# Sending sixteen rows of one load through half of the DMA engines, and riding small inputs in larger transfers

## The chip, the core and the metric

The kernel runs on one core of a Trainium2 chip. The core has a matrix engine (PE, with its weight loads listed apart as PEld), a vector engine (DVE), a scalar engine (ACT), GpSimd (POOL) and a synchronisation engine (SP), and 16 DMA engines that bring data from the chip's memory (HBM) into the on-chip memory (SBUF, 128 partitions or "rows"). Here SP issues nearly all loads, ACT issues three small ones. The metric is the device time of one execution in microseconds (us). The kernel before takes 699.19 us, the median of three runs (698.89 to 699.32).

## The reference

One decode step of a transformer block, all in float32, with batch 2, one query token per sequence, model width 512, 32 heads of 128, a key and value cache of 4096 positions, and a feed-forward layer of width 1376:

```python
mod = (silu(c) @ w_mod).reshape(2, 6, 1, 512)
sa, ca, ga, sb, cb, gb = (mod[:, i] for i in range(6))
h = layernorm(x) * (1 + ca) + sa
q = (h @ wq)                                  # 32 heads
p = softmax(q . k_cache / sqrt(128))
x = x + ga * ((p . v_cache) @ wo)
h = layernorm(x) * (1 + cb) + sb
x = x + gb * (mish(h @ w1 + b1) @ w2)
```

The caches are 2 x 32 x 4096 x 128 floats each, so that K and V together are 268 of the 297 MB that are read. Everything else is weights (wq and wo 8.4 MB each, w_mod 6.3 MB, w1 and w2 2.8 MB each) and a few kilobytes of vectors.

## The kernel before, in words

**Loads.** On the host the inputs are laid out as a list of loads, `stream()`, and each load is an array of 128 rows. K of one head is 8192 columns (32 KB a row), V of one head the same. Three buffers in SBUF take the loads in turn: two of the tag `two` (16384 columns) and one of the tag `one` (12288 columns). The first load (lines 46 and 143) holds the first three modulation weights `m012` and the first two pieces of `wq`, in two transfers. Then K and V come head by head, mostly two heads in one transfer, with a piece of `wq` or `wo` beside every fifth head. The last three loads are cut into smaller transfers (lines 59 to 63): the last piece of `wo` with the fourth modulation `m4`, then V of the last head in three cuts; the third modulation `m3` and `w1` in two halves; `m5` and `w2` in four cuts, the last two of 512 columns (2 KB a row).

**What sets the order.** The order of instructions on each engine is written out by hand. `used(...)` (line 148) issues the next load as soon as the code that reads its buffer's former contents has been written, and at run time the transfer waits on semaphores until those readers are done. A transfer also waits for the transfer that used the same of the eight DMA semaphores eight transfers earlier. All loads stand in SP's one queue.

**Work per head.** DVE multiplies K by q (line 316) and sums (line 319), PE and DVE find the maximum over all rows (lines 324 to 337), ACT takes the exponential (line 339), and PE multiplies by V (line 365, `weighted_v`). V runs behind K by some heads. After four heads the sums are normalised (`head_values`) and multiplied by a piece of `wo` (`project_o`).

**The start.** ACT issues three small transfers of its own, c and x (8 rows each, line 165) and the biases b1 as 128 rows of 12 floats (line 167). PE transposes c (`columns`, line 231), then a matmul at line 263 puts the biases into the accumulator `fps`, and the modulation matmuls follow (`modulation`, line 241).

**The tail.** After the last head's V the attention output is completed (lines 486 to 494), the second normalisation is computed (`centred`, line 194, and `rstd`, line 215), and around it PE computes the modulation `m3` in two halves (lines 499 and 502) and a few idle matmuls (`busy`, line 293), whose result nobody reads. Then follow w1 (line 521), the activation (lines 548 to 556), w2 (line 561), two DVE operations (lines 569 and 570) and the store of the result (line 571).

Of the kernel before, what the change touches and what calls it, by code (L numbers as in the profile page):

```python
# [8 lines left out]
F32 = mybir.dt.float32  # L9
# [4 lines left out]
P = 128  # L14
WIDTHS = (384, 384, 352, 256)
CHUNKS = [(g, j) for j in range(3) for g in range(4) if WIDTHS[g] > P * j]
HEADS = 32
HC = 4
BIG = 8192
W = 2048  # L20
SIZES = {
    "k": BIG, "v": BIG, "wq": W, "wo": W, "m012": 3 * W, "m3": W, "m4": W, "m5": W,
    "w1": 4 * sum(WIDTHS), "w2": 512 * len(CHUNKS),
}
AHEAD = (14, 22)


def stream():

    behind, pieces = {}, [("k", 0)]
    for h in range(1, HEADS):
        pieces.append(("k", h))
        if h not in AHEAD:
            behind[h] = len(behind)
            pieces.append(("v", behind[h]))
    left = list(range(len(behind), HEADS))
    pieces += [("v", h) for h in left[:-1]]

    extra = {}
    for c in range(2, HEADS // HC):
        at = (pieces.index(("k", HC * c)) - 1) // 5 * 5
        extra[at] = [("wq", c), ("wo", c - 2)]
    extra[60] = [("wo", HEADS // HC - 2)]
    loads = [[([("m012", 0), ("wq", 0), ("wq", 1)], (3 * W, 2 * W))]]
    n = 0
    while n < len(pieces):
        m = 1 if n % 5 == 0 else 2
        keys = pieces[n : n + m]  # L50
        if keys[0] == ("v", left[0]) and m == 2:
            loads.append([([key], (BIG,)) for key in keys])
        else:
            keys = keys + (extra.pop(n, []) if m == 1 else [])
            loads.append([(keys, (sum(SIZES[kind] for kind, _ in keys),))])
        n += m
    assert not extra and len(loads) % 3 == 0
    last = HEADS - 1
    loads += [
        [([("wo", HEADS // HC - 1), ("m4", 0)], (2 * W,)), ([("v", last)], (BIG // 2, BIG // 4, BIG // 4))],  # L60
        [([("m3", 0), ("w1", 0)], (W, 2 * sum(WIDTHS), 2 * sum(WIDTHS)))],
        [([("m5", 0), ("w2", 0)], (W, 6 * 512, 3 * 512, 512, 512))],
    ]
    return loads, behind, left
# [3 lines left out]
def kernel(  # L68
# [1 line left out]
    tc: tile.TileContext,  # L70
    loads: list,
    head: bass.AP,
    b1c: bass.AP,
    behind: dict,
    left: list,
    out: bass.AP,
# [9 lines left out]
    nc = tc.nc  # L86
    ctx.enter_context(tc.manual_schedule())
    B = 2
    DH = 128
    D = 512  # L90
    G = D // P
    R = P // G
    TB = R // B
    H = HEADS
    NS = BIG // (B * DH)
    NJ = 3
    EPS = 1e-5
    SCALE = DH ** -0.5
    NCH = len(CHUNKS)

    const = ctx.enter_context(tc.tile_pool(name="const", bufs=1))
    work = ctx.enter_context(tc.tile_pool(name="work", bufs=2))
# [18 lines left out]
    def take(t, keys):  # L121
        lo = 0
        for kind, n in keys:
            part = t[:, lo : lo + SIZES[kind]]
            lo += SIZES[kind]
            if kind in "kv":
                (k_t if kind == "k" else v_t)[n] = part.rearrange("p (b j d) -> p b j d", b=B, d=DH)
            elif kind in ("wq", "wo"):
                (wq_t if kind == "wq" else wo_t)[n] = part.rearrange("p (k n) -> p k n", k=G)
            else:  # L130
                w_t[kind] = part.rearrange("p (k n) -> p k n", k=NCH if kind == "w2" else G)

    w_t = {}
    done = set()

    def load(n):

        t = room(n)
        lo = 0
        for keys, srcs in loads[n]:  # L140
            take(t[:, lo:], keys)
            for src in srcs:
                nc.sync.dma_start(out=t[:, lo : lo + src.shape[-1]], in_=src)  # L143
                lo += src.shape[-1]

    loaded = 0
# [1 line left out]
    def used(*keys):  # L148

        nonlocal loaded  # L150
        done.update(keys)
        while loaded < len(loads) and (
            loaded < 3 or all(key in done for keys, _ in loads[loaded - 3] for key in keys)
        ):
            load(loaded)
            loaded += 1
# [1 line left out]
    used()  # L158


    cq = work.tile([P, P], F32, tag="xn", name="cq", bufs=1)
    xq = const.tile([P, P], F32, name="xq")
    for t, src in ((cq, head[0]), (xq, head[1])):
        nc.gpsimd.memset(t, 0.0)
        nc.scalar.dma_start(out=t[::TB, :], in_=src)
    bias = const.tile([P, NCH + 1], F32, name="bias")
    nc.scalar.dma_start(out=bias, in_=b1c)
    nc.scalar.preload_act_table_set("natural_log_exp_and_others")
    ident = const.tile([P, P], F32, name="ident")
    make_identity(nc, ident)  # L170
# [3 lines left out]
        out=fold, in_=ident.rearrange("p (g r) -> p r g", g=G), axis=AX.X, op=ALU.add  # L174
# [3 lines left out]
        out=mean_w, in0=fold[:, None, :].to_broadcast([P, G, R]), scalar1=1.0 / D, scalar2=None, op0=ALU.mult  # L178
# [55 lines left out]
    def modulation(name, n, t, ps=None, ks=range(G)):  # L234


        if ps is None:
            ps = wide_ps(f"modps{name}")[:, : n * P].rearrange("p (m n) -> p m n", m=n)
        for k in ks:
            for g in range(G):  # L240
                nc.tensor.matmul(  # L241
                    ps[R * g : R * (g + 1)],
                    lhsT=ct[:, k, :],
                    rhs=t[:, k, :].rearrange("p (m n) -> p m n", m=n)[:, :, P * g : P * (g + 1)],
                    start=(k == 0),
                    stop=(k == G - 1),
                )
        return ps
# [8 lines left out]
    xn = work.tile([P, P], F32, tag="xn", name="xn", bufs=1)  # L257
    xc, var, rs = centred(xq, "a")
# [1 line left out]
    nc.vector.tensor_scalar(out=xn, in0=xc, scalar1=y0, scalar2=y1, op0=ALU.mult, op1=ALU.mult)  # L260

    fps = psum.tile([P, 512], F32, tag="att2", name="fps", bufs=1)[:, : NJ * G * B]
    nc.tensor.matmul(fps, lhsT=ident, rhs=bias[:, :, None].to_broadcast([P, NJ * G, B]), start=True, stop=False, skip_group_check=True)  # L263

    ps = modulation("0", 3, w_t["m012"])
    hq = const.tile([P, P], F32, name="hq")
# [1 line left out]
    nc.vector.tensor_tensor(out=hq, in0=ps[:, 0, :], in1=hq, op=ALU.add)  # L268
    mod = {}

    def keep(m, ps):
        mod[m] = const.tile([P, P], F32, name=f"mod{m}")
        nc.scalar.copy(mod[m], ps)

    keep(2, ps[:, 2, :])
    hps = columns(hq, "hps")
    hc = const.tile([P, G, B], F32, name="hc")
    nc.vector.tensor_copy(hc, hps)  # L278
# [14 lines left out]
    def busy(n):  # L293

        for lo in range(0, n, 2):
            cols = P * min(2, n - lo)
            nc.tensor.matmul(ov[1][:, :cols], lhsT=ident, rhs=e_t[0][0].rearrange("p c m -> p (c m)")[:, :cols], start=True, stop=True)
# [130 lines left out]

    project_q(0)
    project_q(1)  # L430
    used(("m012", 0), ("wq", 0), ("wq", 1))
    for h in range(H):
        products(h)
        if h:
# [61 lines left out]
    def add_x(total):  # L496
        nc.vector.scalar_tensor_tensor(x2, xg, 1.0, xq, op0=ALU.mult, op1=ALU.add, accum_out=total)

    mps3 = modulation("3", 1, wm3, ks=(0, 1))

    def more_work():
        modulation("3", 1, wm3, mps3, (2, 3))
        busy(1)

    xc, var, rs = centred(x2, "b", add_x, more_work)
    busy(6)
    nc.vector.tensor_tensor(out=m4, in0=xc, in1=m4, op=ALU.mult)
    y0, y1 = rstd(var, rs)
    nc.scalar.activation(xc, m4, AF.Copy, scale=y0)
# [37 lines left out]

    nc.vector.tensor_scalar(out=f[:, 0], in0=hid, scalar1=30.0, scalar2=None, op0=ALU.min)
    nc.scalar.activation(f[:, 0], f[:, 0], AF.Exp)
    keep(5, gps[:, 0, :])  # L550
    busy(6)
    nc.vector.scalar_tensor_tensor(f[:, 1], f[:, 0], 2.0, f[:, 0], op0=ALU.add, op1=ALU.mult)
    nc.vector.tensor_scalar(out=f[:, 2], in0=f[:, 1], scalar1=2.0, scalar2=None, op0=ALU.add)
# [20 lines left out]
def _lay_out(np, a):  # L574


    def rows(w):

        return w.reshape(-1, P, w.shape[-1]).transpose(1, 0, 2)

    def q_rows(v):

        return v.reshape(2, 4, P).transpose(1, 0, 2).reshape(8, P)

    B, H, S, DH = a["A_k_cache"].shape
    kv = {
        kind: a[n].reshape(B, H, P, -1).transpose(1, 2, 0, 3).reshape(H, P, -1)
        for kind, n in (("k", "A_k_cache"), ("v", "A_v_cache"))
    }
    wq = rows(a["A_wq"]).reshape(P, 4, 8, 512).transpose(2, 0, 1, 3).reshape(8, P, -1)  # L590
    wo = a["A_wo"].reshape(8, 4, P, 512).transpose(0, 2, 1, 3).reshape(8, P, -1)
    wm = rows(a["w_mod"])
    w1 = rows(a["B_w1"])
    starts = np.cumsum((0,) + WIDTHS)
    b1c = np.zeros((P, 12), a["B_b1"].dtype)
    w2 = np.zeros((P, len(CHUNKS), 512), a["B_w2"].dtype)
    for n, (g, j) in enumerate(CHUNKS):
        f0 = starts[g] + P * j
        f1 = min(f0 + P, starts[g + 1])
        b1c[: f1 - f0, n] = a["B_b1"][f0:f1]  # L600
        w2[: f1 - f0, n] = a["B_w2"][f0:f1]

    pieces = {**kv, "wq": wq, "wo": wo, "m012": [wm[:, :, :1536]], "w1": [w1], "w2": [w2]}
    for n in (3, 4, 5):
        pieces[f"m{n}"] = [wm[:, :, 512 * n : 512 * (n + 1)]]
    arrays = {
        "head": np.stack([q_rows(a["c"]), q_rows(a["A_x"])]),
        "b1c": b1c,
    }
    for n, parts in enumerate(stream()[0]):  # L610
        for i, (keys, widths) in enumerate(parts):
            row = np.concatenate([pieces[kind][m].reshape(P, -1) for kind, m in keys], axis=1)
            cuts = np.split(row, np.cumsum(widths)[:-1], axis=1)
            for j, t in enumerate(cuts):
                arrays[f"load{n}_{i}_{j}"] = np.ascontiguousarray(t)
    return arrays
# [24 lines left out]
```

## Time and profile before

| | |
|---|---|
| median of three runs | 699.19 us |
| the profiled execution's own time | 698.83 us |
| its span, first to last instruction | 697.0 us |
| DVE busy | 595.8 us (85%) |
| PE busy | 308.2 us (44%) |
| ACT busy | 43.7 us (6%) |
| read from HBM | 297.22 MB, 426 GB/s over the span |

The profiled execution is 1.8 us longer than its span (what lies before the first and after the last instruction), and 0.36 us shorter than the median of the runs. In the windows and pages quoted below, "DMA share" is the mean busy share of the 16 DMA engines: 1.00 means that all 16 had a packet under way all of the time. A packet of a load is one row of it. Queue q1 carries what SP issues, q10 what ACT issues, and the rows marked "instruction" carry the engines' own program.

### The profile page before, as it was taken

What the parts mean: (1) busy time and instruction counts of PE and PEld (TensorE: products, weight loads), DVE (VectorE), ACT (ScalarE), POOL (GpSimd) and SP (SyncE); (2) the same over time, 40 slices, a digit from 0 to 9 for tenths busy, and PEclk for the clock granted to TensorE, in tenths of its full rate; (3) what the DMA queues carried; (4) which work ended last, traced back from release to release, by engine and by line L of the source; (5) the groups of instructions that cost most, each with busy time, mean ns of one, the idle gap of its engine ahead of it and who ended that gap; (6) DMA issues with size and microseconds to landing.
All of it is one profiled execution on the core that took longest, in us unless ns stands there. A gap on an engine that the chain in (4) does not pass through costs nothing.

```text
span 697.0 us, 4072 instructions
## 1 busy us (share of the span) xinstructions
PE 308.2 (44%) x1692; PEld 107.0 (15%) x1692; DVE 595.8 (85%) x218; ACT 43.7 (6%) x176; POOL 4.4 (1%) x22
## 2 busy tenths in 40 slices
PE   2913343523453722843034831644043832226686
PEld 1300011100110200310011200211010300002234
DVE  3399999959999769999999789999999689999501
ACT  1100000000000000010000100000000100000001
POOL 2000000000000000000000000000000000000000
PEclk9966656776556765695665865986556975666799
DMA  9999999999999999999999999999999999999996
GB/s 383 453 429 417 427 459 411 448 429 416 454 432 425 438 425 428 448 430 433 429 444 426 432 440 417 446 432 429 444 423 440 430 425 440 429 420 432 422 422 269
DMA packets 7842, 297.48 MB, mean 427 GB/s; under 512 B 1016, under 2 KB 1040, under 8 KB 1424
## 3 DMA queue, kind: packets, MB, share of 16 engines
q1 hardware_dynamic: 7648, 297.21, 98.9%
q8 instruction: 13, 0.21, 0.1%
q10 hardware_dynamic: 176, 0.01, 0.0%
q14 instruction: 5, 0.04, 0.0%
HBM read 297.22 MB, written 0.00 MB: 426 GB/s over the span
## 4 chain that ended last, share of the span: by engine, by line
DVE 72%; DMA 24%; PE 2%; issue 1%; POOL 0%; SPq 0%; ACT 0%; DVEq 0%; POOLq 0%
DVE s L319 35%; DVE two L316 25%; DMA two<-in_load 22%; DVE one L316 10%; DMA bias<-in_b1c 2%; DVE d L326 1%; PE qps L288 1%; PE modps L241 1%; DVE m L324 1%; DVE m L337 0%; DVE pick L357 0%; SPq L143 0%; DVE pick L356 0%; PE fps L263 0%; ACT q L291 0%
## 5 line engine op out<-in xcount | busy, mean ns | idle before, releaser
L316 DVE TENSOR_TENSOR two<-two,q 128x8192 f32<-128x8192 f32 x24 | 208.5, 8687 | 37.1 <-DMA two<-in_load 37.1
L319 DVE TENSOR_REDUCE s<-two 128x64 f32<-128x8192 f32 x24 | 208.2, 8675 | 0.0
L365 PE MATMUL ov<-two,e 128*32 128x512 f32 x864 | 148.0, 847 | 134.1 <-DMA two<-in_load 81.9
L331 PE MATMUL mt<-d,ones 128*128 128x256 f32 x64 | 28.6, 536 | 130.3 <-DVE d L326 130.3
L316 DVE TENSOR_TENSOR one<-one,q 128x8192 f32<-128x8192 f32 x8 | 69.5, 8685 | 7.9 <-ACT q L291 7.9
L365 PEld LDWEIGHTS ov<-two,e 128*32 128x32 f32 x864 | 33.8, 149 | 233.4 <-issue 110.3
L319 DVE TENSOR_REDUCE s<-one 128x64 f32<-128x8192 f32 x8 | 69.4, 8676 | 0.0
L339 ACT ACTIVATE e<-s,m 128x32 f32<-128x32 f32 x64 | 20.1, 314 | 483.0 <-DVE m L337 483.0
L288 PE MATMUL qps<-one,hc 128*128 128x512 f32 x96 | 45.0, 624 | 0.0
L365 PE MATMUL ov<-one,e 128*32 128x512 f32 x160 | 28.1, 867 | 32.8 <-ACT e L339 17.1
L331 PEld LDWEIGHTS mt<-d,ones 128*128 128x128 f32 x64 | 12.0, 235 | 153.5 <-DVE d L326 108.9
L348 PE MATMUL l<-l,ones 128*128 128x8 f32 (+2 forms) x18 | 5.4, 370 | 63.4 <-ACT e L339 63.4
L288 PEld LDWEIGHTS qps<-one,hc 128*128 128x128 f32 x96 | 18.9, 201 | 24.4 <-issue 24.1
L348 PEld LDWEIGHTS l<-l,ones 128*128 128x128 f32 x18 | 4.5, 312 | 68.9 <-ACT e L339 68.5
L337 DVE TENSOR_REDUCE m<-mt 128x2 f32<-128x256 f32 x32 | 13.4, 418 | 1.4 <-PE mt L331 1.4
L326 DVE TENSOR_TENSOR d<-ident,m 128x256 f32<-128x256 f32 x32 | 13.6, 425 | 1.1
L365 PEld LDWEIGHTS ov<-one,e 128*32 128x32 f32 x160 | 6.3, 154 | 52.0 <-ACT e L339 17.9
L288 PE MATMUL qps<-two,hc 128*128 128x512 f32 x32 | 14.0, 595 | 0.3 <-DVE hc L278 0.3
L387 PE MATMUL otp<-pick,o 128*128 128x8 f32 (+2 forms) x72 | 10.0, 264 | 7.6 <-DVE m L324 4.7
L291 ACT ACTIVATE q<-qps 128x512 f32<-128x512 f32 x16 | 9.4, 594 | 52.2 <-PE qps L288 52.2
L339 ACT ACTIVATION_READ_ACCUMULATOR e<-s,m 128x1 f32 x64 | 12.0, 187 | 0.0
L387 PEld LDWEIGHTS otp<-pick,o 128*128 128x128 f32 x72 | 9.2, 200 | 14.8 <-ACT o L379 9.1
(105 smaller groups left out, 95.0 us busy)
## 6 DMA issues: line engine op xcount, KB each, us to landing
one<-in_load SPq DMA_DIRECT2D x6, 6144.0 KB, 31.8
one<-in_load SPq DMA_DIRECT2D x6, 4096.0 KB, 29.7
two<-in_load SPq DMA_DIRECT2D x2, 4096.0 KB, 24.7
two<-in_load SPq DMA_DIRECT2D x3, 2048.0 KB, 14.8
one<-in_load SPq DMA_DIRECT2D x1, 5120.0 KB
two<-in_load SPq DMA_DIRECT2D x1, 3072.0 KB
two<-in_load SPq DMA_DIRECT2D x3, 1024.0 KB, 20.7
one<-in_load SPq DMA_DIRECT2D x2, 1376.0 KB
```

The costliest lines, as they stand in the source:

```text
L241: nc.tensor.matmul(ps[R * g : R * (g + 1)], lhsT=ct[:, k, :], rhs=t[:, k, :].rearrange("p (m n) -> p m n", m=n)[:, :, P * g : P * (g + 1)] ...
L288: nc.tensor.matmul(ps, lhsT=hc[:, k, b : b + 1].to_broadcast([P, P]), rhs=wq_t[ch][:, k, :], start=(k == 0), stop=(k == G - 1))
L291: nc.scalar.activation(q_t[ch][:, b].rearrange("p h d -> p (h d)"), ps, AF.Copy, scale=SCALE)
L316: nc.vector.tensor_tensor(out=k_t[h], in0=k_t[h], in1=qv, op=ALU.mult)
L319: nc.vector.tensor_reduce(out=s_t[h], in_=k_t[h], axis=AX.X, op=ALU.add)
L326: nc.vector.tensor_tensor(out=d, in0=ident[:, None, :].to_broadcast([P, B, P]), in1=m_t[h][:, 0:2, None].to_broadcast([P, B, P]), op=ALU.mult,
L331: nc.tensor.matmul(mps[h], lhsT=ones, rhs=d, start=True, stop=True)
L337: nc.vector.tensor_reduce(out=m[:, 2:4], in_=mps[h], axis=AX.X, op=ALU.max, negate=True)
L339: nc.scalar.activation(e_t[i][b][:, :, M * i + 4 * b : M * i + 4 * b + 4], s_t[h][:, b].rearrange("p (c m) -> p c m", m=4), AF.Exp, bias=m ...
L348: nc.tensor.matmul(lps[n][:, x], lhsT=ones, rhs=l_t[n][:, x], start=True, stop=True)
L365: nc.tensor.matmul(ov[bank][R * g : R * (g + 1), :], lhsT=e_t[h % HC][b][:, c, :], rhs=v_t[h][:, b, 4 * c : 4 * c + 4, :].rearrange("p m d ...
L387: nc.tensor.matmul(tps[:, x], lhsT=o_t[m], rhs=pick_t[n][:, m, x], start=(m == 0), stop=(m == 3),)
```

## The change

Four edits are made together.

1. **Uneven rows.** The transfer that brings the last piece of `wo` and `m4` (128 rows of 16 KB) is cut by rows into three: rows 0 to 111, rows 112 to 119, rows 120 to 127. The one of 112 rows is to go through all 16 DMA engines, 7 rows each, and each of the two of 8 rows through the lower eight engines alone, one row each.
2. **Biases.** `b1` is no longer a transfer of its own; its 12 columns stand between `m012` and `wq` in the first load, whose first transfer grows from 6144 to 6156 columns. `wq` so begins 48 bytes later in its SBUF row.
3. **c and x.** Both come in one transfer of 8 rows of 256 floats, into one tile `first` that is cleared by one memset, instead of two and two.
4. **Third modulation.** `m3` and the first half of `w1` come in one transfer. In the tail the whole of modulation 3 now stands behind the variance matmul, and the idle matmuls are distributed otherwise. (`mod5` takes the place of a finished tile, to save room.)

```diff
-    "k": BIG, ..., "w1": 4 * sum(WIDTHS), "w2": 512 * len(CHUNKS),
+    "b1": 12, "w1": 4 * sum(WIDTHS), "w2": 512 * len(CHUNKS),
 }
+UNEVEN = (("wo", HEADS // HC - 1),)
...
-    loads = [[([("m012", 0), ("wq", 0), ("wq", 1)], (3 * W, 2 * W))]]
+    loads = [[([("m012", 0), ("b1", 0), ("wq", 0), ("wq", 1)], (3 * W + 12, 2 * W))]]
...
-        [([("m3", 0), ("w1", 0)], (W, 2 * sum(WIDTHS), 2 * sum(WIDTHS)))],
+        [([("m3", 0), ("w1", 0)], (W + 2 * sum(WIDTHS), 2 * sum(WIDTHS)))],
...
             for src in srcs:
-                nc.sync.dma_start(out=t[:, lo : lo + src.shape[-1]], in_=src)
+                cuts = (0, 112, 120, P) if keys[0] in UNEVEN else (0, P)
+                for r0, r1 in zip(cuts, cuts[1:]):
+                    nc.sync.dma_start(out=t[r0:r1, lo : lo + src.shape[-1]], in_=src[r0:r1])
...
-    for t, src in ((cq, head[0]), (xq, head[1])):
-        nc.gpsimd.memset(t, 0.0)
-        nc.scalar.dma_start(out=t[::TB, :], in_=src)
-    bias = const.tile([P, NCH + 1], F32, name="bias")
-    nc.scalar.dma_start(out=bias, in_=b1c)
+    first = const.tile([P, 2 * P], F32, name="first")
+    nc.gpsimd.memset(first, 0.0)
+    nc.scalar.dma_start(out=first[::TB, :], in_=head)
...
-    nc.tensor.matmul(fps, lhsT=ident, rhs=bias[:, :, None].to_broadcast([P, NJ * G, B]), ...)
+    nc.tensor.matmul(fps, lhsT=ident, rhs=w_t["b1"].to_broadcast([P, NJ * G, B]), ...)
...
-    mps3 = modulation("3", 1, wm3, ks=(0, 1))
-
-    def more_work():
-        modulation("3", 1, wm3, mps3, (2, 3))
-        busy(1)
-
-    xc, var, rs = centred(x2, "b", add_x, more_work)
-    busy(6)
+    busy(3)
+    xc, var, rs = centred(x2, "b", add_x, lambda: busy(4))
+    busy(1)
+    mps3 = modulation("3", 1, wm3)
```

How the change moves instructions is seen in three places. In all rows the number behind a name is only a running number. First SP's queue in the tail, before (`two_1263` holds two heads of V, `two_1302` the last piece of `wo` with `m4` and then the last head of V, `one_1327` holds `m3` and `w1`, `two_1388` holds `m5` and `w2`; DMAHW is one of the eight DMA semaphores):

```order
L143 DMA two_1302<-in_load_0_0 128x4096 [waits DMAHW0_49,DVE_49,PE_49]
L143 DMA two_1302<-in_load_1_0 128x4096
L143 DMA two_1302<-in_load_1_1 128x2048
L143 DMA two_1302<-in_load_1_2 128x2048
L143 DMA one_1327<-in_load_0_0 128x2048 [waits DMAHW1_49,PE_49]
L143 DMA one_1327<-in_load_0_1 128x2752
L143 DMA one_1327<-in_load_0_2 128x2752 [waits DMAHW2_49]
L143 DMA two_1388<-in_load_0_0 128x2048 [waits DMAHW3_49,PE_49]
```

and the same place of the changed kernel:

```order
L146 DMA two_1297<-in_load_0_0 112x4096 [waits DMAHW6_49,DVE_49,PE_49]
L146 DMA two_1297<-in_load_0_0 8x4096 x2
L146 DMA two_1297<-in_load_1_0 128x4096
L146 DMA two_1297<-in_load_1_1 128x2048
L146 DMA two_1297<-in_load_1_2 128x2048 [waits DMAHW7_49]
L146 DMA one_1324<-in_load_0_0 128x4800 [waits DMAHW0_49,PE_49]
L146 DMA one_1324<-in_load_0_1 128x2752 [waits DMAHW1_49]
L146 DMA two_1384<-in_load_0_0 128x2048 [waits DMAHW2_49,PE_49]
```

One transfer of 128 rows has become one of 112 and two of 8, and two transfers of one load have become one of 4800 columns; the waits on the eight semaphores have moved to other transfers.

Second, PE at the start, before (`cps` is c turned to columns, `fps` takes the biases, `modps` the first three modulations, DMAHW3 is the transfer of the biases and DMAHW0 the first transfer of the first load):

```order
L231 MATMUL cps<-ident,cq 128x8 [waits DMAHW1_49,Pool_49]
L204 MATMUL mean_a<-rs_a,mean_w 128x1 [waits DVE_49]
L212 MATMUL var_a<-rs_a,mean_w 128x1 [waits DVE_49,PE_49]
L263 MATMUL fps<-bias,ident 128x24 [waits DMAHW3_49]
L241 MATMUL modps_132<-two_69,ct 32x384 [waits DMAHW0_49,Pool_49]
```

and now:

```order
L232 MATMUL cps<-ident,first 128x8 [waits DMAHW1_49,Pool_49]
L205 MATMUL mean_a<-rs_a,mean_w 128x1 [waits DVE_49]
L213 MATMUL var_a<-rs_a,mean_w 128x1 [waits DVE_49,PE_49]
L264 MATMUL fps<-two_69,ident 128x24 [waits DMAHW0_49]
L242 MATMUL modps_127<-two_69,ct 32x384 [waits Pool_49]
```

The bias matmul waits for the first transfer of the first load, in place of the biases' own transfer.

Third, PE in the tail, before (`mean_b` and `var_b` are the two sums of the second normalisation, `modps_1468` is modulation 3, `ov_105` takes the idle matmuls):

```order
L403 MATMUL xps<-two_1302,ot_168 32x128 x4
L241 MATMUL modps_1468<-one_1327,ct 32x128 x8
L204 MATMUL mean_b<-rs_b,mean_w 128x1
L241 MATMUL modps_1468<-one_1327,ct 32x128 x8
L297 MATMUL ov_105<-e_0_159,ident 128x128
L212 MATMUL var_b<-rs_b,mean_w 128x1
L297 MATMUL ov_105<-e_0_159,ident 128x256 x3
L231 MATMUL h2ps<-ident,hq 128x8
```

and now:

```order
L404 MATMUL xps<-two_1297,ot_163 32x128 x4
L298 MATMUL ov_100<-e_0_154,ident 128x256
L298 MATMUL ov_100<-e_0_154,ident 128x128
L205 MATMUL mean_b<-rs_b,mean_w 128x1
L298 MATMUL ov_100<-e_0_154,ident 128x256 x2
L213 MATMUL var_b<-rs_b,mean_w 128x1
L298 MATMUL ov_100<-e_0_154,ident 128x128
L242 MATMUL modps_1479<-one_1324,ct 32x128 x16
L232 MATMUL h2ps<-ident,hq 128x8
```

Modulation 3 has moved behind `var_b` in one piece, and idle matmuls stand where its halves stood.

More of the change, by code (lines that the diff above doesn't have):

```diff
@@ L22 @@
     "k": BIG, "v": BIG, "wq": W, "wo": W, "m012": 3 * W, "m3": W, "m4": W, "m5": W,
-    "w1": 4 * sum(WIDTHS), "w2": 512 * len(CHUNKS),
+    "b1": 12, "w1": 4 * sum(WIDTHS), "w2": 512 * len(CHUNKS),
 }
+UNEVEN = (("wo", HEADS // HC - 1),)
 AHEAD = (14, 22)
@@ L72 @@
     head: bass.AP,
-    b1c: bass.AP,
     behind: dict,
@@ L130, in take @@
             else:
-                w_t[kind] = part.rearrange("p (k n) -> p k n", k=NCH if kind == "w2" else G)
+                w_t[kind] = part.rearrange("p (k n) -> p k n", k={"b1": NCH + 1, "w2": NCH}.get(kind, G))
     w_t = {}
@@ L158 @@
     used()
-    cq = work.tile([P, P], F32, tag="xn", name="cq", bufs=1)
-    xq = const.tile([P, P], F32, name="xq")
-    for t, src in ((cq, head[0]), (xq, head[1])):
-        nc.gpsimd.memset(t, 0.0)
-        nc.scalar.dma_start(out=t[::TB, :], in_=src)
-    bias = const.tile([P, NCH + 1], F32, name="bias")
-    nc.scalar.dma_start(out=bias, in_=b1c)
+    first = const.tile([P, 2 * P], F32, name="first")
+    nc.gpsimd.memset(first, 0.0)
+    nc.scalar.dma_start(out=first[::TB, :], in_=head)
+    cq = first[:, 0:P]
+    xq = first[:, P : 2 * P]
     nc.scalar.preload_act_table_set("natural_log_exp_and_others")
@@ L262 @@
     fps = psum.tile([P, 512], F32, tag="att2", name="fps", bufs=1)[:, : NJ * G * B]
-    nc.tensor.matmul(fps, lhsT=ident, rhs=bias[:, :, None].to_broadcast([P, NJ * G, B]), start=True, stop=False, skip_group_check=True)
+    nc.tensor.matmul(fps, lhsT=ident, rhs=w_t["b1"].to_broadcast([P, NJ * G, B]), start=True, stop=False, skip_group_check=True)
     ps = modulation("0", 3, w_t["m012"])
@@ L269, with keep @@
     mod = {}
-    def keep(m, ps):
-        mod[m] = const.tile([P, P], F32, name=f"mod{m}")
+    def keep(m, ps, pool, **kw):
+        mod[m] = pool.tile([P, P], F32, name=f"mod{m}", **kw)
         nc.scalar.copy(mod[m], ps)
-    keep(2, ps[:, 2, :])
+    keep(2, ps[:, 2, :], const)
     hps = columns(hq, "hps")
@@ L430 @@
     project_q(1)
-    used(("m012", 0), ("wq", 0), ("wq", 1))
+    used(("m012", 0), ("b1", 0), ("wq", 0), ("wq", 1))
     for h in range(H):
@@ L549 @@
     nc.scalar.activation(f[:, 0], f[:, 0], AF.Exp)
-    keep(5, gps[:, 0, :])
+    keep(5, gps[:, 0, :], work, tag="xc", bufs=1)
     busy(6)
@@ L601, in _lay_out @@
         w2[: f1 - f0, n] = a["B_w2"][f0:f1]
-    pieces = {**kv, "wq": wq, "wo": wo, "m012": [wm[:, :, :1536]], "w1": [w1], "w2": [w2]}
+    pieces = {**kv, "wq": wq, "wo": wo, "m012": [wm[:, :, :1536]], "b1": [b1c], "w1": [w1], "w2": [w2]}
     for n in (3, 4, 5):
@@ L606, in _lay_out @@
     arrays = {
-        "head": np.stack([q_rows(a["c"]), q_rows(a["A_x"])]),
-        "b1c": b1c,
+        "head": np.ascontiguousarray(np.concatenate([q_rows(a["c"]), q_rows(a["A_x"])], axis=1)),
     }
```

## The prediction

> **What bounds the kernel now.** I read the page's slices of the span and its DMA queues first (the columns of the latter are packets, megabytes, share of 16 engines' span).
>
> ```profile
> DMA  9999999999999999999999999999999999999996
> q1 hardware_dynamic: 7648, 297.21, 98.9%
> q8 instruction: 13, 0.21, 0.1%
> q10 hardware_dynamic: 176, 0.01, 0.0%
> q14 instruction: 5, 0.04, 0.0%
> ```
>
> SP's loads alone fill the 16 DMA engines for 98.9% of the span. DVE, busy for 85%, leads the page's shares of the chain, so I asked the chain in order of time (start, length, what) whether DVE or the loads set the end.
>
> ```profile
> 2.79 12.11 DMA bias<-in_b1c
> ...
> 138.93 27.90 DMA two<-in_load
> ...
> 653.77 20.74 DMA two<-in_load
> 674.53 18.52 DMA two<-in_load
> 693.09 0.47 PE yps L561 x8
> 693.66 0.30 DVE y L569
> 693.98 0.29 DVE y L570
> ```
>
> Four times in the middle, first at 138.93, DVE stands still for some 28 us because its data is not there, and the last 39.3 us before 693.09 are two waits for loads. The windows then tell whether the DMA engines ever pause (last columns: granted PE clock, DMA share, GB/s):
>
> ```profile
> 1.70:9.80 8.10, 0.57 (x2) 0.50 (x2) 3.60 (x8) 1.46 (x2) 2.84 (x13) 1.00 0.99 392
> 175.00:350.00 175.00, 74.75 (x342) 24.62 (x342) 164.16 (x50) 10.38 (x44) 0.00 (x0) 0.67 1.00 432
> 0.00:690.00 690.00, 305.22 (x1604) 104.80 (x1604) 595.19 (x216) 43.74 (x176) 4.36 (x22) 0.71 1.00 430
> 689.00:690.00 1.00, 0.23 (x2) 0.00 (x0) 0.00 (x0) 0.00 (x0) 0.00 (x0) 1.00 0.86 338
> 690.00:691.00 1.00, 0.96 (x36) 0.99 (x40) 0.00 (x0) 0.00 (x0) 0.00 (x0) 1.00 0.64 252
> 691.00:692.00 1.00, 0.75 (x30) 0.48 (x24) 0.00 (x0) 0.00 (x0) 0.00 (x0) 1.00 0.39 137
> 692.00:692.70 0.70, 0.70 (x32) 0.56 (x24) 0.00 (x0) 0.00 (x0) 0.00 (x0) 1.00 0.17 64
> ```
>
> They don't pause: 1.00 up to 690. The time is the bytes of each engine at 432 / 16 = 27.0 GB/s, plus 4.4 us of tail. But the engines don't end together: from 689 to 692.7 the share falls from 0.86 to 0.17. The missing engine time is 0.14 + 0.36 + 0.61 + 0.7 x 0.83 = 1.69 us, and no distribution of the same bytes can gain more than these 1.69 us (0.24%).
>
> **Who ends last.** The records of single packets behind these rows tell it. On one engine each packet starts 3 ns before the recorded end of the one before, so the packets fall apart into 16 strings that I could follow from 1.8 us to the end. An engine's string has its place by the eight 512-byte packets of the 8-row transfer of c:
>
> ```profile
> q10 hardware_dynamic: 8, 0.00, 2.7%
> q8 instruction: 1, 0.02, 6.2%
> ```
>
> The first row is the window 6.0 to 6.5 (c's eight packets, on eight different strings: these I call the lower eight). The second is 63.06 to 64.08 (1.02 us), where one program packet of 16 KB holds one engine for 0.062 x 16 x 1.02 = 1.01 us; the packet behind it takes half a microsecond longer too, so that its string is 1.5 us behind for the rest of the run. The strings, grouped from the records (us):
>
> ```
> lower  16 KB program at   8 KB program at   last load packet
>  a     63.1, 555.9                          692.35
>  b     124.3, 632.2                         692.43
>  c                        135.8, 509.5      691.41
>  d                        216.9, 630.0      690.89
>  e                        636.8             690.16
>  f g h                                      689.65 689.63 689.38
> upper
>  i     237.6, 683.3                         692.60
>  j     181.8, 664.5                         692.50
>  k     511.6                                691.71
>  l     307.8                                691.17
>  m n   438.4; 375.5                         691.08 691.03
>  o p                                        690.18 689.74
> ```
>
> The last window agrees: 0.17 x 16 x 0.7 = 1.9 us, against 0.60 + 0.50 + 0.43 + 0.35 for i, j, b, a. Who served two 16 KB program packets ends last, and two of these four are lower engines. (A thirteenth falls at 691.2 on l, when l has no data left.) One reservation: i and a lower string ran within 0.02 us of each other until 237.6, so i's side is likely, not certain.
>
> **Uneven rows.** A row of 16 KB takes 16,384 / 27.0 = 0.61 us. The upper eight lose one of eight rows of this load, -0.61. The lower eight carry 7 + 1 + 1, so +0.61, and two more completion packets of some 0.01 us: +0.62. Nothing hides it, since these engines never pause. a and b move to 692.97 and 693.05, i and j to 691.99 and 691.89: the last arrival moves from i to b, by 693.05 - 692.60 = +0.45.
>
> **Biases, and the merged transfers.** Per engine 8 packets of 48 bytes and a completion go. The page of 1.0 to 9.7 prices ACT's packets:
>
> ```profile
> q10 hardware_dynamic: 54, 0.01, 0.6%
> ```
>
> 0.006 x 16 x 8.7 / 54 = 0.015 us each, and 9 x 0.015 = 0.14 at most; a 48-byte packet has 0.011 in the records, 0.008 of it for itself, so 0.06 at least. Eight rows are 48 bytes longer: 384 / 27.0 = +0.014. m3 and half of w1 as one transfer save 8 packet starts and a completion, about 9 x 0.005 = 0.05 (the distance of two 2 KB packets in the records, 0.080, is 0.005 above 2,048 / 27.0). c and x together save a further 0.01 on the lower eight. Sum -0.06 to -0.20; I take -0.10, near the smaller rows.
>
> ```profile
> 14.93 0.62 PE L263 MATMUL fps<-bias,ident 128*128 128x24 f32 x2 [3.01 <-DMA bias<-in_b1c]
> 15.48 5.35 PE L241 MATMUL modps<-two,ct 128*32 128x384 f32 x32
> 30.02 8.69 DVE L316 TENSOR_TENSOR one<-one,q 128x8192 f32<-128x8192 f32 x1 [7.85 <-ACT q L291]
> ```
>
> The biases' own transfer holds PE until 14.93, though the first transfer's 3.15 MB are nearly in by 9.8 (8.1 us x 392 GB/s = 3.18 MB) and, with the spread of the engines, at about 11. PE and DVE so start up to 3.9 us sooner. I cost it at nothing: DVE then waits that much longer at 138.93, a wait of 27.90 us. Its price without this cover is a gain of 3.9.
>
> `wq` now lands 48 bytes off. No row here has such a load. From below, nothing; from above, all of the first load (8 x 40 KB per engine, 12.1 us) at half speed, +12.1. The nearest row is that of the 48-byte packets, which cost 0.002 us more than 4-byte completions for 44 bytes, close to full rate, so I take 0. [...]
>
> **The tail.** Modulation 3 now stands in series and waits for half of w1 too:
>
> ```profile
> 679.04 0.65 PE L241 MATMUL modps<-one,ct 128*32 128x128 f32 x16
> 681.43 0.35 DVE L510 SCALAR_TENSOR_TENSOR hq<-xc_b,rs_b,modps 128x128 f32<-128x128 f32 x1
> 683.66 0.97 PEld L521 LDWEIGHTS w1ps<-one,h2t 128*32 128x32 f32 x16 [0.32 <-DMA one<-in_load]
> 688.16 0.20 DVE L556 TENSOR_TENSOR actt<-f 128x22 f32<-128x22 f32 x1
> 690.04 1.52 PE L561 MATMUL yps<-two,actt 128*32 128x128 f32 x48 [0.81 <-DMA two<-in_load]
> 693.09 0.42 PE L561 MATMUL yps<-two,actt 128*32 128x128 f32 x8 [0.21 <-DMA two<-in_load]
> ```
>
> Both halves are 2 x 0.65 = 1.3 us of PE; if all of it delayed line 510, the activation would be ready at 688.36 + 1.3 = 689.7, still before w2's first cut reaches PE (690.04, and later with b). So nothing, with 0.3 us of cover left in the worst case. SP issues the two added transfers, and its new waits are for transfers that are done some 20 us before the data behind them is due on the engines: nothing.
>
> **Sum.** +0.45 - 0.10 = +0.35. In the profiled execution's own time 698.83 + 0.35 = 699.18; the median of the runs is 0.36 above that execution, so 699.19 + 0.35 = 699.5. About 0.2%, or 1.4 us, is what a measurement of this kernel can tell from no change, so I call this the same.
>
> **Rivals.**
> *The split does what it could do* (17%): if the strings that end last are upper ones, or program packets fall on other engines in the changed program, the last arrival falls by up to 0.61, and 699.19 - 0.61 - 0.10 = 698.5. For it: i and j are the last two. Against: a and b, 0.17 us behind i.
> *The rows are not moved* (6%): the 8-row transfers use other engines than c's, and the ends stay: 699.1.
> *Unaligned rows* (6%, slower): the 12.1 us of the first load lie on all engines with no cover. From 9% above its length on (1.05 / 12.1) the total passes 0.2%; a quarter longer gives 699.5 + 3.0 = 702.5. For it: no load before was off a 256-byte boundary. Against: the 48-byte row.
> *The early start counts* (3%, faster): 699.5 - 3.9 = 695.6. Against: the share of 1.00 until 690; DVE is not the bound.
> *Each queued transfer costs a pause* (1%, faster): one fewer is issued in all (two of ACT's and one of SP's go, two come). From the page's rows the price is small: the 1.1% of the span that q1 doesn't fill are 7.7 us, and the tail (4.4), the first 1.8 and the uneven end (1.7) use them up; were all 7.7 pauses between 53 loads, one would be 0.15, and the total 699.4. [...]
>
> **How the numbers follow.** My forecast has the remaining 67%. The range leaves out the unaligned rows at their larger prices, the early start and the pauses (10%): from 698.5 less the 0.2 us that single runs scatter, 698.3, to 699.5 + 0.2 (if i is a lower string, 692.60 + 0.62, so +0.52 in place of +0.35) + 0.8 for a small share of the unaligned price, 700.5. Faster by over 0.2%: early start and a larger price of pauses, 3 + 1 = 4%. Slower: 6%. Within: 90%.
>
> **What would show it.** The DMA share stays 1.00 to about 690 and falls in two steps, since the lower eight now end some 1.2 us later against the upper; over 691 to 693 it should show fewer engines for longer. The wait of `fps` ends at about 11 and DVE starts near 26. Line 556 ends before 689.8 and the last `yps` matmuls start at about 693.4. I am wrong if the last arrival comes before 692.6 (then program packets or sides are not as read), if `wq`'s arrival is late by more than a microsecond against the 15.6 of the records, or if the DMA share falls below 1.00 before 689.

## The result, and the profile after

The changed kernel takes 707.87 us (median of four runs, 707.21 to 709.37) against 699.23 us for the kernel before, timed on the same chip: a ratio of 1.0127, with a 95% interval from 1.011 to 1.0145. It is 8.6 us slower. The forecast was 699.5 us with a range up to 700.5, so it was wrong, and on the side to which it had given 6%. The profiled execution takes 707.85 us (span 706.1), 9.02 us more than that of before.

Where the 9 us lie is not seen in the row that the prediction leaned on. First the slices of the page of before (40 slices of 17.4 us), in GB/s:

```profile
GB/s 383 453 429 417 427 459 411 448 429 416 454 432 425 438 425 428 448 430 433 429 444 426 432 440 417 446 432 429 444 423 440 430 425 440 429 420 432 422 422 269
```

and the same of after, with the DMA engines' busy tenths above it and the loads' queue under it:

```profile
DMA  8999999999999999999999999999999999999996
GB/s 355 440 453 409 427 460 406 438 446 435 420 431 446 424 431 438 434 424 438 438 416 443 438 421 433 446 414 440 435 419 444 432 421 455 420 432 420 272 399 260
q1 hardware_dynamic: 7520, 297.22, 98.8%
```

The engines are as busy as before (98.8%, before 98.9%; all nines but the ends). Only the rate tells: the third slice from the end moves 272 GB/s in place of 422, and the first 355 in place of 383. The windows give both places more sharply. Columns: length, busy us of PE, PEld, DVE, ACT and POOL, granted PE clock, DMA share, GB/s. Before (the first load stands in the prediction, 0.99 and 392):

```profile
658.00:672.00 14.00, 12.02 (x136) 4.67 (x132) 0.29 (x1) 0.76 (x2) 0.00 (x0) 0.87 0.99 418
672.00:690.00 18.00, 15.53 (x168) 9.40 (x160) 4.00 (x19) 2.47 (x10) 0.42 (x1) 0.98 1.00 417
```

After, with the falling end of the run below:

```profile
1.70:9.80 8.10, 0.56 (x2) 0.50 (x2) 3.36 (x8) 1.46 (x2) 2.79 (x12) 1.00 0.91 341
0.00:657.00 657.00, 274.04 (x1299) 88.27 (x1299) 590.50 (x194) 40.19 (x164) 3.89 (x20) 0.70 1.00 430
658.00:672.00 14.00, 9.59 (x64) 2.10 (x56) 0.00 (x0) 0.59 (x1) 0.00 (x0) 0.74 1.00 217
672.00:690.00 18.00, 15.44 (x130) 9.42 (x130) 2.10 (x9) 0.74 (x4) 0.42 (x1) 0.67 1.00 412
698.00:699.00 1.00, 1.00 (x6) 0.71 (x4) 0.22 (x2) 0.09 (x1) 0.00 (x0) 1.00 0.80 313
699.00:700.00 1.00, 0.96 (x30) 0.80 (x33) 0.00 (x0) 0.00 (x0) 0.00 (x0) 1.00 0.52 199
700.00:701.00 1.00, 0.77 (x31) 0.50 (x22) 0.00 (x0) 0.00 (x0) 0.00 (x0) 1.00 0.29 102
701.00:702.00 1.00, 1.00 (x32) 0.73 (x32) 0.00 (x0) 0.00 (x0) 0.00 (x0) 1.00 0.05 18
```

From 658 to 672, where the load with the uneven rows goes through, the rate is half (217 GB/s) at a share of 1.00. The packet records of queue q1 say why both can be: the packets themselves take longer. (Sums over 16 engines, us per engine; of the loads between 640 and 690.)

```
                          before           after
16 KB packets, 256        9.86             16.35     +6.49
  one of them             0.61 (one 1.10)  0.61 to 1.88, 170 of them over 0.9
32 KB packets over 1.5    none             14 of 239, up to 2.42: +0.85
first load, last end      10.68            11.64     +0.96
```

A packet that takes twice as long counts as busy for twice as long, so the share stays at 1.00 while the rate halves. 6.49 + 0.85 + 0.96 = 8.3 of the 9.02 us. Most of the rest is the end of the run, which is less level: up to the last load packet at 701.76 the windows lack 0.20 + 0.48 + 0.71 + 0.71 = 2.1 us of engine time, before (up to 692.60) 1.6.

The chain of waits in order of time (start, length, what) ends as before, with two waits for loads, both longer (20.74 became 26.14, 18.52 became 20.93):

```profile
655.18 26.14 DMA two<-in_load
681.34 20.93 DMA two<-in_load
702.31 0.47 PE yps L558 x8
702.87 0.30 DVE y L566
703.20 0.29 DVE y L567
```

### The profile page after: what moved, and what is told of

Its sections match the earlier page's. It is cut to its first block, busy times and chain, and to the rows that moved or that the text cites. A ratio compares the mean times of both kernels' runs of the same rounds, so it can differ in the third digit from the quotient of the medians.

```text
span 706.1 us, 4071 instructions
## 1 busy us (share of the span) xinstructions
PE 311.2 (44%) x1694; PEld 108.2 (15%) x1694; DVE 595.9 (84%) x218; ACT 43.4 (6%) x176; POOL 4.3 (1%) x21
## 3 DMA queue, kind: packets, MB, share of 16 engines
q1 hardware_dynamic: 7520, 297.22, 98.8%
## 4 chain that ended last, share of the span: by engine, by line
DVE 66%; DMA 28%; PE 3%; issue 1%; SPq 0%; ACT 0%; DVEq 0%; POOL 0%; POOLq 0%
DVE s L320 32%; DMA two<-in_load 27%; DVE two L317 23%; DVE one L317 9%; PE qps L289 2%; DVE d L327 1%; DMA first<-in_head 1%; PE modps L242 1%; DVE m L325 1%; DVE m L338 0%; DVE pick L358 0%; SPq L146 0%; DVE pick L357 0%; PE mean_a L205 0%; PE fps L264 0%
## 5 line engine op out<-in xcount | busy, mean ns | idle before, releaser
L366 PE MATMUL ov<-two,e 128*32 128x512 f32 x864 | 151.8, 867 | 140.3 <-DMA two<-in_load 84.1
L289 PE MATMUL qps<-one,hc 128*128 128x512 f32 x96 | 42.6, 596 | 0.0
```

The lines of the kernel that those rows point to most:

```text
L289: nc.tensor.matmul(ps, lhsT=hc[:, k, b : b + 1].to_broadcast([P, P]), rhs=wq_t[ch][:, k, :], start=(k == 0), stop=(k == G - 1))
L366: nc.tensor.matmul(ov[bank][R * g : R * (g + 1), :], lhsT=e_t[h % HC][b][:, c, :], rhs=v_t[h][:, b, 4 * c : 4 * c + 4, :].rearrange("p m d ...
```

## The experiments

What the experiments are to tell apart, in short: the loss is in the uneven rows, or in the first load; if in the rows, it is the one transfer more, or the rows' source, or the place in SBUF where they land together.

**Even rows.** All of the change without the uneven rows.

```diff
-UNEVEN = (("wo", HEADS // HC - 1),)
+UNEVEN = ()
```

> The changed kernel with all 128 rows of the last wo and m4 in one transfer again; the other three edits stay. Theory R (the rows): in the changed kernel the load rate falls to about 220 GB/s from 658 to 672 us, where the three row pieces are under way, and that costs about 8.1 of the 8.7 us; then this kernel takes 699.8 us (699.2, plus some 1.0 for the slower first load, less 0.1 to 0.4), and the rate stays near 430 GB/s to 690. Rival Q (the merged transfer of m3 and w1 and the moved semaphore waits hold SP's queue back): 706 to 708 us, with the dip still there.

Measured: 700.62 us against 699.17, ratio 1.0026 (1.0011 to 1.0041). Its windows:

```profile
1.70:9.80 8.10, 0.57 (x2) 0.50 (x2) 0.98 (x6) 1.46 (x2) 2.86 (x12) 1.00 0.92 335
658.00:672.00 14.00, 12.45 (x136) 4.74 (x134) 0.55 (x3) 0.75 (x2) 0.00 (x0) 0.86 0.99 417
```

The late stretch is at full rate again, the early one is not. So the rows cost some 7.3 us (707.87 - 700.62), and 1.4 us remain, for which the early window points at the first load. I had expected 699.8, 0.8 less: the first load cost more in this run (its last packet in by 12.00, before 10.68) than the 1.0 us that I had read from the profile of the changed kernel.

**The rows alone.** The kernel before with nothing but the three cuts.

```diff
-                nc.sync.dma_start(out=t[:, lo : lo + src.shape[-1]], in_=src)
+                cuts = (0, 112, 120, P) if keys[0] == ("wo", HEADS // HC - 1) else (0, P)
+                for r0, r1 in zip(cuts, cuts[1:]):
+                    nc.sync.dma_start(out=t[r0:r1, lo : lo + src.shape[-1]], in_=src[r0:r1])
```

> The kernel before with only the cut of the last wo and m4 into 112, 8 and 8 rows. Theory R: 699.2 + 8.1 = 707.3 us (706.5 to 708). Rival Q: 699.5, the sum of the prediction for the rows alone (+0.45).

Measured: 706.54 us against 699.17, ratio 1.0105 (1.0091 to 1.0118), and the half rate in the same place with an undisturbed start:

```profile
1.70:9.80 8.10, 0.57 (x2) 0.50 (x2) 3.31 (x7) 1.46 (x2) 2.82 (x13) 1.00 1.00 394
658.00:672.00 14.00, 7.62 (x60) 1.76 (x52) 0.00 (x0) 0.58 (x1) 0.00 (x0) 0.87 0.98 201
```

The rows alone cost 7.4 us. With the 1.45 of the run before this makes 8.8, against 8.6 for the whole change: the two causes add up.

**112 rows and 16.** The same with one transfer of 16 rows in place of two of 8.

```diff
-                cuts = (0, 112, 120, P) if keys[0] == ("wo", HEADS // HC - 1) else (0, P)
+                cuts = (0, 112, P) if keys[0] == ("wo", HEADS // HC - 1) else (0, P)
```

> The kernel before with the same load cut into 112 and 16 rows: every engine has 7 rows and then 1, 8 in all as before. [...] Rival R2 (the two transfers of 8 rows are the slow part, because 8 engines write into a few neighbouring rows): 699.2 to 700 us.

Measured: 706.72 us, ratio 1.0105 (1.009 to 1.0119).

```profile
658.00:672.00 14.00, 7.69 (x64) 1.77 (x56) 0.00 (x0) 0.59 (x1) 0.00 (x0) 0.87 0.98 224
```

The same as with two transfers of 8. That rows go through the lower engines alone, on which the prediction had spent its working, makes no difference that is seen. What this run doesn't separate is the 112 rows from the last 16, which land side by side in rows 112 to 127 here too. The packet records do so in part: of this run's 256 packets of 16 KB, the first 112 to start take 1.18 us in the median, before 0.61, which is 4.0 us more per engine; the other 144 (mostly the 16 rows and the half of V behind them) add 2.6, and the 32 KB packets ahead 0.75. So the 112 rows are slow from their start, and the 16 rows have a part in the loss.

**Even rows, and a first transfer of whole 256-byte steps.** The biases take 64 columns in place of 12, so that a row is 24,832 bytes, 97 x 256.

```diff
...
-    "b1": 12, "w1": 4 * sum(WIDTHS), "w2": 512 * len(CHUNKS),
+    "b1": 64, "w1": 4 * sum(WIDTHS), "w2": 512 * len(CHUNKS),
-    loads = [[([("m012", 0), ("b1", 0), ("wq", 0), ("wq", 1)], (3 * W + 12, 2 * W))]]
+    loads = [[([("m012", 0), ("b1", 0), ("wq", 0), ("wq", 1)], (3 * W + 64, 2 * W))]]
...
```

> As the first of these kernels (128 rows in one transfer), and the biases take 64 columns in place of 12, so that each row of the first transfer has 24,832 bytes, a multiple of 256, and wq begins at a multiple of 256 bytes. Theory U (rows off a 256-byte boundary made the first transfer end 1.0 us later): 0.8 to 1.1 us faster than the first kernel, near 698.9, and a load rate near 390 GB/s from 1.7 to 9.8 us. Rival V (something else in the start, such as the one transfer of c and x, or chance): the same as the first kernel within 0.3 us, and 341 GB/s again.

Measured: 699.44 us against 699.17, ratio 1.0004 (0.9996 to 1.0013).

```profile
1.70:9.80 8.10, 0.57 (x2) 0.50 (x2) 1.36 (x8) 1.46 (x2) 2.88 (x12) 1.00 1.00 392
25.81 8.69 DVE L317 TENSOR_TENSOR one<-one,q 128x8192 f32<-128x8192 f32 x1 [8.07 <-DMA one<-in_load]
```

The start is whole again and the second loss is gone (700.62 - 699.44 = 1.18 us, against 0.8 to 1.1 expected). What is left of the change, the early start, the merged transfers and modulation 3 in series, can't be told from no change. The second row is the timeline: DVE starts K at 25.81, 4.2 us sooner than before, and nothing comes of it.

**Where the rows land.** The row cuts had now cost 7.4 us for the same bytes. My idea from here on was that the rate of a transfer depends on the rows of SBUF in which its packets land, and not on its bytes alone. I tried this first in the kernel's own load, in halves:

```diff
...
+                cuts = (0, 64, P) if keys[0] == ("wo", HEADS // HC - 1) else (0, P)
...
```

> The kernel before with the last wo and m4 cut into rows 0 to 63 and 64 to 127. Each engine then has 4 rows of either half, 8 in all. [...] Rival N (seven rows for an engine are the trouble, since 7 isn't a part of 8): 699.2. Rival T (each transfer more costs its own pause): 699.2 plus half of what two more transfers cost with 112, 8 and 8 rows, 702.9.

Measured: 706.77 us against 699.29, ratio 1.0108 (1.0094 to 1.0121).

```profile
658.00:672.00 14.00, 7.18 (x60) 1.61 (x52) 0.00 (x0) 0.59 (x1) 0.00 (x0) 0.87 0.98 222
```

Halves, two equal transfers, cost 7.5 us. It is not the unevenness, and not the number seven (rival N).

```diff
...
+                cuts = (0, 96, P) if keys[0] == ("wo", HEADS // HC - 1) else (0, P)
...
```

> The same with rows 0 to 95 and 96 to 127, six and two rows for an engine. [...] Rival N: 699.2. Rival T: 702.9.

Measured: 707.65 us, ratio 1.0117 (1.0103 to 1.0131), 8.4 us.

```profile
658.00:672.00 14.00, 7.64 (x60) 1.75 (x52) 0.00 (x0) 0.59 (x1) 0.00 (x0) 0.87 1.00 209
```

As a control, the same load in two transfers, cut by columns, 128 rows each:

```diff
-        [([("wo", HEADS // HC - 1), ("m4", 0)], (2 * W,)), ...
+        [([("wo", HEADS // HC - 1), ("m4", 0)], (W, W)), ...
```

> A control: the same load cut by columns into two transfers of 2048 columns, all 128 rows in both. [...] Rival T: 702.9, as for the cuts by rows.

Measured: 699.40 us, ratio 1.0000 (0.9991 to 1.001).

```profile
658.00:672.00 14.00, 12.52 (x140) 4.64 (x132) 0.29 (x1) 0.75 (x2) 0.00 (x0) 0.89 1.01 421
```

One transfer more costs nothing, so rival T falls too; cut by rows it costs 7.5.

The other loss has three candidates. The padded row had changed three things: the length of a row, the place of `wq` in SBUF, and where the rows start in HBM. Here only the last is mended: the changed kernel with even rows, its rows still 24,624 bytes and `wq` still 48 bytes off, but the source laid out at a pitch of 6208 columns (24,832 bytes).

```diff
...
+                src = src[:, :w]
...
-                arrays[f"load{n}_{i}_{j}"] = np.ascontiguousarray(t)
+                arrays[f"load{n}_{i}_{j}"] = np.ascontiguousarray(np.pad(t, ((0, 0), (0, -t.shape[1] % 64))))
...
```

> The changed kernel with 128 rows in one transfer, and the source of the first transfer laid out with 6208 columns a row, of which 6156 are loaded: each source row begins at a multiple of 256 bytes, its length is still 24,624 bytes, and wq still lands 48 bytes off. Theory U1 (the place where a source row begins is what slows the first transfer): 699.4, as with the biases padded. Rival U2 (the length, or the place in the on-chip memory): 700.6, as without padding.

Measured: 699.44 us against 699.29, ratio 1.0001 (0.9992 to 1.0009).

```profile
1.70:9.80 8.10, 0.58 (x3) 0.52 (x3) 3.57 (x8) 1.46 (x2) 2.79 (x12) 1.00 1.01 393
690.28 0.20 DVE L554 TENSOR_TENSOR actt<-f 128x22 f32<-128x22 f32 x1
691.28 2.61 PE L559 MATMUL yps<-two,actt 128*32 128x128 f32 x88
```

The start is whole, so it was the rows' starting places in the source; the length of the row and the landing place of `wq` cost nothing. (The last two rows are used further below.)

**The collision by itself.** The kernel before with seven transfers of 32 KB rows put at its very start, all from the same source, into rows that differ in number and in spacing. Nothing reads their data before the second load overwrites it; the time is longer by what they take.

```diff
...
+            src = loads[1][0][1][0]
+            for rows, step in ((10, 1), (10, 12), (16, 1), (16, 7), (64, 1), (112, 1), (128, 1)):
+                nc.sync.dma_start(out=saved[0][0 : (rows - 1) * step + 1 : step, :BIG], in_=src[0:rows])
...
```

> A look at single transfers with nothing beside them: the kernel before, with seven more transfers at its very start, each waiting for the last, all from the same array in HBM with rows of 32 KB, into the buffer that then receives the first head's K: 10 rows into rows 0 to 9; the same 10 into every twelfth row; 16 into rows 0 to 15; the same 16 into every seventh row; 64, 112 and 128 into rows from 0 on. Their results are overwritten and the total is longer by these transfers and their waits, some 40 us. [...] Rival H (the source or the number of rows sets the rate, not where they land): the two transfers of 10 rows take the same time, and the two of 16.

Measured: 758.51 us against 699.07 (one run each), 59.4 us longer and not the 40 expected. Each of these windows lies inside one of the seven, in their order (the last three leave out the first and last packets):

```profile
1.70:5.80 4.10, 0.00 (x0) 0.00 (x0) 0.66 (x4) 0.00 (x0) 2.91 (x13) 1.00 0.54 81
8.90:10.80 1.90, 0.66 (x3) 0.60 (x3) 0.95 (x5) 0.00 (x0) 0.00 (x0) 1.00 0.43 138
12.10:16.20 4.10, 0.00 (x0) 0.00 (x0) 0.51 (x3) 0.00 (x0) 0.00 (x0) 1.00 0.84 120
18.90:21.20 2.30, 0.00 (x0) 0.00 (x0) 0.00 (x0) 0.00 (x0) 0.00 (x0) 1.00 0.70 199
24.00:33.00 9.00, 0.00 (x0) 0.00 (x0) 0.00 (x0) 0.00 (x0) 0.00 (x0) 1.00 0.86 175
36.00:48.00 12.00, 0.00 (x0) 0.00 (x0) 0.00 (x0) 0.00 (x0) 0.00 (x0) 1.00 0.97 251
54.00:62.00 8.00, 0.00 (x0) 0.00 (x0) 0.00 (x0) 0.00 (x0) 0.00 (x0) 1.00 0.95 410
```

and the records of their packets (us, one 32 KB packet):

```
rows                    one packet
10 neighbours           8 of 3.05 to 4.01, 2 of 2.43 to 2.51
10, 12 apart            1.28 to 1.85
16 neighbours           3.37 to 3.91
16, 7 apart             1.55 to 2.04
64                      median 2.57, up to 2.66
112                     median 2.12, from 1.47 to 3.08
128                     median 1.21; the first on an engine up to 2.13
```

The same ten source rows are about twice as fast 12 apart (1.28 to 1.85 us) as side by side (2.43 to 4.01): the landing place decides, and a cause in the source falls. (That they take more than 1.21 us does not speak against it: in the transfer of 128 rows, too, the first packets on the engines took up to 2.13.) Of 10 neighbours eight packets are slow (3.05 to 4.01) and two less slow (2.43 to 2.51); of 16 neighbours all are slow (3.37 to 3.91), of the 16 rows 7 apart none took more than 2.04. A transfer of 64 rows runs at twice the time per packet all along (2.57 us), one of 112 at 1.75 times (2.12). So a transfer of 112 rows is slow by itself, with nothing beside it. Why rows that land side by side are slower is not shown, since no record names an engine or a row.

**In the kernel, without cuts.** Two further transfers of 8 rows of 16 KB are put behind the uncut load, into columns of its buffer that nothing reads. Once the 16 rows are spread (rows 0, 4 ... 28 and 1, 5 ... 29), once they are neighbours (112 to 119 and 120 to 127, as in the changed kernel).

```diff
+            if keys[0] == ("wo", HEADS // HC - 1):
+                for rows in (slice(0, 29, 4), slice(1, 30, 4)):
+                    nc.sync.dma_start(out=t[rows, 2 * W + BIG : 4 * W + BIG], in_=srcs[0][0:8])
```

> [...] Rival E (what is added is shared by all engines): 262 KB at 430 GB/s, 0.6 us, 699.8. Rival K (any transfer of 8 rows costs what the cut did): over 703.

Measured: 699.27 us against 699.14, ratio 1.0004 (0.9993 to 1.0014). I had expected 700.3, with the lower engines that serve two program packets ending 2 x 0.61 us later.

```profile
658.00:672.00 14.00, 12.64 (x140) 4.69 (x132) 0.29 (x1) 0.76 (x2) 0.00 (x0) 0.87 1.00 420
690.00:691.00 1.00, 0.97 (x33) 1.00 (x37) 0.00 (x0) 0.00 (x0) 0.00 (x0) 1.00 0.82 326
691.00:692.00 1.00, 0.81 (x31) 0.55 (x27) 0.00 (x0) 0.00 (x0) 0.00 (x0) 1.00 0.66 240
```

```diff
-                for rows in (slice(0, 29, 4), slice(1, 30, 4)):
+                for rows in (slice(112, 120), slice(120, 128)):
```

> [...] Rival (where the rows land doesn't matter for 8 rows): the same as with the rows 4 apart.

Measured: 703.32 us against 699.14, ratio 1.0056 (1.004 to 1.0071).

```profile
658.00:672.00 14.00, 11.57 (x128) 4.30 (x116) 0.29 (x1) 0.75 (x2) 0.00 (x0) 0.85 1.00 334
```

The same number of transfers, bytes and source rows: spread, 0.1 us, which can't be told from nothing; neighbours, 4.2 us. The difference lies in the rows where they land. The two profiled executions lie 5.15 us apart (704.08 and 698.93). In this run the 16 KB packets of the stretch take 13.32 us per engine, with spread rows 10.47: 2.85 of the 5.15. The rest is a less level end:

```profile
694.00:695.00 1.00, 0.45 (x3) 0.05 (x1) 0.00 (x0) 0.00 (x0) 0.00 (x0) 1.00 0.50 195
695.00:696.00 1.00, 0.82 (x32) 0.85 (x36) 0.00 (x0) 0.00 (x0) 0.00 (x0) 1.00 0.12 47
```

From 692 to the last load packet at 697.67 the engines lack 3.1 us, with spread rows 1.0 (689 to 692.60): 2.1 more. So sixteen neighbouring rows alone cost over half of what the whole cut costs (4.2 of 7.4 us).

The miss with the spread rows is of another kind. I had kept the prediction's rule that the lower eight DMA engines, which carry the two rows more, would end last. They do carry 18 such rows in place of 16 in the records, but the 16 KB program packets now fall on other engines: as far as the strings can be followed, all four engines that serve two of them (63.0 and 555.9, 133.5 and 632.3, 181.7 and 664.9, 237.5 and 685.5) are upper ones, where before two were lower. Lower and upper end level (692.60 and 692.58), and the share shows it: 0.82 and 0.66 over 690 to 692, before 0.64 and 0.39. The added 1.2 us of the lower engines were filled into slack.

## Why the prediction was wrong

**The load stream is the bound: held**, and so what was lost in it was seen (8.3 us in the packets and the first load, of 9.02 in the time). But the view by which I had meant to see a loss, "share of 1.00 until 690", is blind to a loss of this kind: it stayed at 1.00 over 658 to 690, and fell only at the start.

**Uneven rows, +0.45: the step that failed.** The term was bytes per engine at 27.0 GB/s, the rate of transfers of 128 rows. A transfer of fewer rows, or of rows that land side by side, ran at another rate: the three cuts alone measured +7.4, sixteen times the term, as packets of 16 KB took about 1.2 us in place of 0.61 (the first 112 of them 1.18 in the median, with 112 and 16 rows). That the landing rows set the rate is shown (the same two transfers of 8 rows cost 4.2 us as neighbours and 0.1 spread); the reason is not. I had gone through rivals for who ends last and what a row weighs, and had none for rows of one load that get into each other's way, though every large load in the trace of before has 128 rows, so that it could not vouch for the rate of 112. A bound from above was to be had, as an estimate: this load takes each engine 8 x 0.61 = 4.9 us, and the half of V behind it as much, so at half rate they cost 4.9 to 9.8 us more. The range left this out.

**Unaligned rows, 0 taken, 6% for a slower outcome: the second miss, smaller.** The kind was a rival, the size was neither the forecast's 0 nor the rival's 3.0: it measured 1.2 us (700.62 - 699.44, both for the padded row and for the padded pitch). I had looked for it in `wq`, 48 bytes off in SBUF, which cost nothing; it lies in the rows of the first transfer, whose starts in HBM are 24,624 bytes apart. Their packets take 8.23 us per engine, before 7.96, so most of the second is between packets, not in them (the window's share is 0.91); what happens there is open. Of the signs I had named, `wq` came 0.9 us late (its transfer in by 16.50, before 15.58, behind a first transfer that was 1.0 late), just inside the bound of a microsecond that I had set.

**Who ends last: the reading of before agreed with its last window, its carrying over was not shown.** In the changed kernel the loss hides it; with spread rows the program packets fell on other engines than before. The chance I gave that (part of 17%) was too small for something that differs from program to program, and the term of +0.45 had no ground even without the collision.

**The early start, 0: right.** The timeline of after:

```profile
11.97 0.62 PE L264 MATMUL fps<-two,ident 128*128 128x24 f32 x2
27.06 8.69 DVE L317 TENSOR_TENSOR one<-one,q 128x8192 f32<-128x8192 f32 x1 [7.85 <-ACT q L292]
```

`fps` runs at 11.97 and DVE starts at 27.06, each about 1 us later than I had named, by the late first load; with the mended first load they are 11.67 and 25.81. The cover was misread, though. 27.90 us is how long the chain followed a transfer until it landed, and DVE does not stand still for that long. Its own waits for K up to 657 us (total, number, longest), before:

```profile
DVE two L316 <- DMA two<-in_load: 37.1, 8, 9.1
```

and after:

```profile
DVE two L317 <- DMA two<-in_load: 40.8, 10, 9.4
```

The start that DVE gained, 3.0 us, is found again as 3.7 us more waiting. The cover was 37 us in eight pieces of 9.1 at most, which was enough: the term came out right, the reason given for it did not.

**Biases and merged transfers, -0.10: not contradicted, not measurable.** All of the change without its two faults measures +0.15 to +0.27 us, with intervals of about 0.6 us to each side. The price of a queued transfer, which I had put at near nothing against a rival of 1%, fits: one transfer more, by columns, 699.40 against 699.29, with an interval of 0.6 us to each side.

**The tail, 0: right in the changed kernel**, whose last matmuls wait for loads, but with less cover than is comfortable. In the run with the padded pitch the two rows quoted above show `actt` written at 690.28 and the `yps` matmuls running in one piece of 2.61 us from 691.28: there the loads were no longer waited for, PE set the end, and the activation came 0.8 us after the 689.7 of my worst case. The order of instructions is not the cause, since the run with the padded row has the same one, with `actt` at 688.94 and last matmuls that wait for loads. The runs differ in the granted PE clock while the last eight V matmuls run, which both begin at 675.0: 1.00 with the padded row (first line), where they take 1.06 us, and 0.50 with the padded pitch (second line), where they take 1.94:

```profile
675.00:677.00 2.00, 1.99 (x14) 0.83 (x14) 0.40 (x1) 0.37 (x1) 0.00 (x0) 1.00 1.03 438
675.00:677.00 2.00, 2.00 (x9) 0.34 (x9) 0.00 (x0) 0.00 (x0) 0.00 (x0) 0.50 0.92 394
```

My working of the tail had no term for this. It cost nothing that the median shows (699.44 against 699.29).

**The sign "two steps in the fall of the share"** can't be read: after falls 0.80, 0.52, 0.29, 0.05, by the collision and not by the rows' bytes.

What stays open: how the 112 rows are dealt over the engines was not seen (the records don't name an engine or a row), nor how the 7.4 us divide between them and the 16 neighbours, nor why rows side by side are slower, so the exact size of a cut could not be worked out beforehand. And no version here beats the kernel before: the four that lose nothing (the change without uneven rows, padded in either way, the cut by columns, the spread rows) all lie within 0.1% of it.

## What to carry to other kernels

Cut a load by columns, not by rows: with all 128 rows in each transfer a second one cost nothing (699.40 us against 699.29), while a cut of a 2 MB load at row 64, 96 or 112 cost 7.4 to 8.4 us. Where a stream of loads is the bound, read its rate (GB/s) and the time of one packet beside the busy share, since slow packets count as busy: 217 GB/s went with a share of 1.00. And before a small input rides in front of larger rows, see where that puts the start of the next row in HBM: 48 bytes cost 1.2 us, and padding the row to 97 x 256 bytes took them back (699.44 us, from 700.62).

## What the runs showed of the hardware that was not expected

- The rows that a transfer lands in set its rate. A 32 KB packet took 1.21 us in the median in a transfer of 128 rows, 2.12 in one of 112 and 2.57 in one of 64; into 10 rows side by side eight took 3.05 to 4.01 and two 2.43 to 2.51, and the same ten, 12 rows apart, 1.28 to 1.85. In the kernel two more transfers of 8 rows of 16 KB cost 4.2 us as neighbours and 0.1 spread. The reason is not shown.
- The loss reaches the transfer ahead: 14 rows of 32 KB of it took over 1.5 and up to 2.42 us in place of 1.21.
- Rows that start 24,624 bytes apart in HBM slowed a 3.15 MB transfer by 1.0 us (1.3 in the run with even rows); the landing place 48 bytes off and the odd length did not (699.44 us with both kept, against 699.29).
- On which DMA engines the 16 KB program packets fall differs between programs, as far as their strings can be followed (engines with two of them: two lower and two upper before, four upper with the spread rows), and with it which engines end last.
